# Four edits to the weight conversion and the attention steps in the first token group of an attention and MoE kernel

## The chip, the cores and the metric

The kernel runs on one core of a Trainium2 chip. The metric is device time in microseconds (us), from one launch that does everything, as the median of several runs.

## The reference

Linear attention with decay runs over blocks of 64 tokens, for 4 batches and 8 heads of 64 features; its output, laid out as 3072 tokens by 512 features, then goes through a two-layer network with a squared ReLU.

```python
for b in range(nb):                      # nb = 768 / 64 blocks
    intra = einsum('bhic,bhjc->bhij', qb, kb) * Dmask       # lam ** (i - j), lower triangle
    intra = einsum('bhij,bhjd->bhid', intra, vb)
    inter = einsum('bhid,bhde->bhie', qb * lam_pow, kv_state)
    out[:, :, sl] = intra + inter
    kv_state = lam_block * kv_state + einsum('bhsd,bhse->bhde', kb * rev_pow, vb)
x = out.transpose(0, 2, 1, 3).reshape(3072, 512)
h = x @ w_in                             # 512 x 2048
g = maximum(h, 0) ** 2
return g @ w_out                         # 2048 x 512
```

## The kernel before, in words

Attention works in chunks t of 128 tokens (24 of them, 6 to a batch), each with two blocks of 64. The network works in token groups m of four chunks (512 tokens). All matrix products of the network are taken in three parts, from a rounded upper and a remaining lower part of each factor: weights `wh` and `wl`, inputs `xh` and `xl`, squared activations `gh` and `gl`.

The order of the instructions of each engine is written out by hand: what the code says first, an engine does first, and it waits there when its input is not ready. Only the order between engines is left to semaphores.

The program has four stages. A prologue does the attention of chunks 0 to 3. Then token group m = 0 runs 16 steps f = 0 to 15. In step f, TensorE (PE) computes `hidden(0, f)` (12 matmuls, L587), then `project` of the step before (12 matmuls, L623 to L628). Meanwhile the weights of slot u = f + 2 are converted on the fly, since they come from memory as 64-bit words that have to be split in two: `first_hi` and `first_lo` on ScalarE (ACT, L210 and L215) write a working buffer `A`; `clamp`, `shift`, `sign` and `rounded` on VectorE (DVE, L223, L227, L234, L240) turn it into the rounded weight; `upper` (ACT, L246) copies it to `wh`; `lower` (DVE, L249) subtracts that from `A` and writes `wl`. `A` has two buffers, used in turn by slots.

The activations of a step go from PSUM through ACT: `positive` (L594) and two squares (L598, L603); then `rest` (DVE, L608) writes `gl`, and with it the PSUM bank of that step's h comes free.

In every fourth step (f = 2, 6, 10, 14; step 2 of four) PE also does a `burst` between `hidden` and `project`: it computes the scores of chunk t + 1, the results of chunk t and the new state terms of chunk t + 1, all as small 64 x 64 matmuls (L386), into one bank of `h` and two banks b0 and b1. `masked` (DVE, L477 or L484) multiplies scores by the decay mask and writes `a`; `keep` copies results into xh and xl of the next group; `fade` (ACT, L514, four instructions) multiplies the old state by the decay; `advance` (DVE, L300 with st) adds the new term from PSUM onto it, once for each block b of the chunk. The chain of a chunk is advance(t, 0), fade(t, 1), advance(t, 1). Chunk 4 is the first in this loop. Its scores and terms stand in `att`, two banks that `look` fills at the end of step 0. Those banks are given back before step 2, and b0 and b1 of burst(5) take their place.

GpSimd (POOL) scales k and q (`prep_k`, L471; `prep_q`, L466). `turn` (L256) is a one-element copy on POOL that reads a piece of `wl` that DVE has just written, and so holds POOL until then. SyncE (SP) issues the loads: `wload(u)` for the raw weights, `load_kq` and `load_v` for a chunk.

After m = 0 come m = 1 and two pairs of groups with seven products in place of eight; nothing of the weight conversion is left there.

Of the kernel before, what the change touches and what calls it, by code (L numbers as in the profile page):

```python
# [7 lines left out]
F32 = mybir.dt.float32  # L8
# [7 lines left out]
P = 128  # L16
# [6 lines left out]
DM = H * D  # L23
# [19 lines left out]
def body(ctx: ExitStack, tc: tile.TileContext, qT, kT, kvq, lam, w, out):  # L43
    nc = tc.nc
    const = ctx.enter_context(tc.tile_pool(name="const", bufs=1))
    dram = ctx.enter_context(tc.tile_pool(name="dram", bufs=1, space=bass.MemoryType.DRAM))
    wk = ctx.enter_context(tc.tile_pool(name="wk", bufs=2))
    small = ctx.enter_context(tc.tile_pool(name="small", bufs=1))
# [27 lines left out]
    def warm(n):  # L76
        w_ = two_banks(ps_a, "att")
        for _ in range(n):
            nc.tensor.matmul(  # L79
                w_[:, 0], st[:, 0, 0].rearrange("p a b -> p (a b)"),  # L80
                st[:, 0:2].rearrange("p n c a b -> p (n c a b)"), start=True, stop=True,
            )

    warm(4)

# [85 lines left out]

    wh = const.tile([P, 2 * NF, DM], F32R, name="wh")
    wl = const.tile([P, 2 * NF, DM], F32R, name="wl")

# [8 lines left out]

    raw, cv, hole = {}, {}, None

# [21 lines left out]
    def first_hi(u):  # L207
        r = raw.pop(u).bitcast(U32).rearrange("p (n two) -> p n two", two=2)
        A = wk.tile([P, r.shape[1]], U32, name="A")
        nc.scalar.activation(A.bitcast(F32), r[:, :, 1].bitcast(F32), AF.Abs)  # L210
        cv[u] = r[:, :, 0], r[:, :, 1], A

# [29 lines left out]
    def flat(t, u):  # L242
        return t[:, pieces(u)].rearrange("p a b -> p (a b)")

    def upper(u):
        nc.scalar.copy(flat(wh, u), cv[u][2].bitcast(F32))  # L246

    def lower(u):
        V.tensor_tensor(  # L249
            out=flat(wl, u), in0=cv.pop(u)[2].bitcast(F32), in1=flat(wh, u).bitcast(F32),  # L250
            op=ALU.subtract,
        )

# [6 lines left out]
    for t in range(4):  # L260
        place(t)
        load_kf(t)
        load_all(t)
    wload(1)

# [202 lines left out]
    def prep_k(t):  # L468
        x = chunk[t]["k"]
        y = near.rearrange("p j a c -> p a j c")[:, :, :, T - 1 : T]  # L470
        nc.gpsimd.tensor_tensor(out=x, in0=x, in1=y.broadcast_to([P, NPR, 2, D]), op=ALU.mult)  # L471

    def masked(t):
# [9 lines left out]
        for j in range(2):  # L483
# [4 lines left out]
            )  # L488

    def before_block(n):  # L490
        return st[:, n % 3]

# [175 lines left out]
    def w_parts(i, S):  # L668
        p1, p2 = w_in(2 * i), w_in(2 * i + 1)
        hl = wk.tile([P, 2, 4, HALF], F32R, name="hl", tag="raw")  # L670
        nc.scalar.copy(hl[:, 0], S)
        V.tensor_tensor(out=hl[:, 1], in0=S, in1=hl[:, 0].bitcast(F32), op=ALU.subtract)
        for k, x in enumerate((wh, wl)):
            x = x.bitcast(F32)
            nc.sync.dma_start(
                out=wd[i, :, W11 : W12 + 1, k], in_=x[:, p1].rearrange("p (b n) -> p b n", b=2)
            )
            nc.sync.dma_start(out=wd[i, :, W22, k], in_=x[:, p2, HALF:DM])
            nc.sync.dma_start(out=wd[i, :, WS1 : WS4 + 1, k], in_=hl[:, k].bitcast(F32))
# [174 lines left out]
    copy_qx(2)  # L854
    first_hi(1)
    low[0]()
    load(4)
    load_vx(4)
    early(1, banks())
# [8 lines left out]
    copy_vx(3)  # L868
    low[1]()
    early_news(3)  # L870
    masked(3)
    upper(0)
    copy_qx(3)
    early(2, banks())
    wload(2)
    low[2] = split(2, o[2])
    clamp(1)
    state(3)
    lower(0)
# [22 lines left out]
    for m in range(PLAIN):  # L902
# [6 lines left out]
        for f in range(NF):  # L909
            h = hidden(m, f, *xs_of[m])  # L910
            if m == 0:
# [213 lines left out]
```

## Time and profile before

| | us |
|---|---|
| median of 3 runs | 589.23 (588.75 to 589.6) |
| the profiled execution, its own time | 588.08 |
| its span in the trace | 586.2 |
| PE busy | 572.8 (98%) |
| DVE busy | 323.1 (55%) |
| ACT busy | 317.5 (54%) |
| POOL busy | 66.7 (11%) |

All times below are microseconds from the start of the span. PE's matmuls overlap: one of 128 x 512 is drawn as 0.39 long, and the next starts about 0.23 after it. DVE's and ACT's drawn lengths overlap the next instruction by some 0.06 to 0.1, so the distance between two starts is the price of an instruction. What stands in brackets behind a row is the idle time ahead of it on its engine and what ended it.

### The profile page before, as it was taken

How to read it: one execution, taken by the hardware profiler on the slowest of the kernel's cores; microseconds unless marked ns; L12 is line 12 of the kernel's file. 1: busy time of each engine (PE TensorE's matmuls, PEld its weight loads, DVE VectorE, ACT ScalarE, POOL GpSimd, SP SyncE). 2: the span in 40 equal slices, each digit the busy share in tenths (PEclk: the TensorE clock that was granted, in tenths of full speed). 3: DMA queues.
4: the chain of work that ended last, by engine and by line, in shares of the span. 5: the costliest groups of instructions: out<-in, count | busy, mean ns of one | idle time of the engine just before them, and what ended most of it. 6: DMA issues, size and time to landing. Idle time of an engine off the chain costs nothing.

```text
span 586.2 us, 12793 instructions
## 1 busy us (share of the span) xinstructions
PE 572.8 (98%) x5240; PEld 470.1 (80%) x5240; DVE 323.1 (55%) x587; ACT 317.5 (54%) x594; POOL 66.7 (11%) x87
## 2 busy tenths in 40 slices
PE   8899999999999999999999999999999999999997
PEld 5777887788888888888888888888888888888885
DVE  6899999975767776534344343446433333334222
ACT  3698887976665465445545445634344444444221
POOL 7401202033232000011111101000000000000000
PEclk8999999999999999999999999999999999999999
DMA  8676667346797933856554553300354444411001
GB/s 335 220 283 228 223 217 229 104 128 196 243 364 260 348 130 103 284 164 197 168 166 137 179 173 98 126 1 0 102 168 126 125 122 120 122 50 73 1 0 72
DMA packets 52089, 93.62 MB, mean 160 GB/s; under 512 B 4672, under 2 KB 19520, under 8 KB 52032
## 3 DMA queue, kind: packets, MB, share of 16 engines
q1 hardware_dynamic: 52032, 92.82, 49.5%
q8 instruction: 41, 0.67, 0.4%
q14 instruction: 16, 0.13, 0.1%
HBM read 71.83 MB, written 20.97 MB: 158 GB/s over the span
## 4 chain that ended last, share of the span: by engine, by line
PE 87%; DVE 6%; ACT 3%; issue 2%; DMA 1%; POOL 1%; POOLq 0%; DVEq 0%
PE h L729 26%; PE acc L623 14%; PE acc L628 14%; PE acc L624 13%; PE h L587 11%; PE h L386 4%; PE b L386 3%; DVE A L234 1%; PE att L79 1%; DVE wl L249 1%; DVE A L240 1%; ACT A L210 1%; DVE A L227 1%; DVE A L223 1%; DVE st L500 1%
## 5 line engine op out<-in xcount | busy, mean ns | idle before, releaser
L623 PE MATMUL acc<-wh,gh 128*128 128x512 f32 x384 | 151.7, 395 | 0.0
L624 PE MATMUL acc<-wl,gh 128*128 128x512 f32 x384 | 149.6, 389 | 0.0
L628 PE MATMUL acc<-wh,gl 128*128 128x512 f32 x384 | 149.3, 390 | 0.1
L623 PEld LDWEIGHTS acc<-wh,gh 128*128 128x128 f32 x384 | 72.1, 188 | 16.0 <-issue 0.3
L628 PEld LDWEIGHTS acc<-wh,gl 128*128 128x128 f32 x384 | 72.1, 188 | 15.2
L624 PEld LDWEIGHTS acc<-wl,gh 128*128 128x128 f32 x384 | 72.1, 188 | 14.4
L608 DVE TENSOR_TENSOR gl<-h,gh 128x512 fp32r<-128x512 f32 x48 | 33.1, 689 | 69.7 <-ACT h L603 69.7
L594 ACT ACTIVATE h<-h 128x512 f32<-128x512 f32 x48 | 28.1, 584 | 69.7 <-PE h L587 36.0
L300 DVE TENSOR_TENSOR temp<-h,temp 128x512 f32<-128x512 f32 x48 | 33.0, 688 | 56.9 <-PE h L729 46.8
L729 PE MATMUL h<-wh,ring 128*128 128x512 f32 x224 | 60.0, 390 | 0.0
L594 ACT ACTIVATE temp<-temp 128x512 f32<-128x512 f32 x16 | 10.1, 632 | 88.6 <-DVE temp L300 88.6
L729 PEld LDWEIGHTS h<-wh,ring 128*128 128x128 f32 x224 | 42.0, 188 | 8.9 <-DVE r L300 0.3
L466 POOL TENSOR_TENSOR qs<-set,qpow 128x512 f32<-128x512 f32 (+1 forms) x21 | 26.5, 1260 | 170.7 <-PE b L386 159.2
L587 PE MATMUL h<-xh,wh 128*128 128x512 f32 x128 | 34.6, 392 | 3.0 <-DVE a L484 2.2
L300 DVE TENSOR_TENSOR r<-h,temp 128x512 f32<-128x512 f32 x24 | 16.6, 692 | 34.2 <-PE h L729 33.1
L608 DVE TENSOR_TENSOR gl<-r,gh 128x512 fp32r<-128x512 f32 x24 | 16.6, 690 | 32.9 <-ACT gh L761 32.9
L729 PE MATMUL h<-wl,ring 128*128 128x512 f32 x112 | 34.5, 389 | 0.0
L587 PE MATMUL h<-xh,wl 128*128 128x512 f32 x128 | 34.5, 391 | 0.0
L587 PE MATMUL h<-xl,wh 128*128 128x512 f32 x128 | 34.3, 389 | 0.0
L761 ACT CAST gh<-r 128x512 fp32r<-128x512 f32 x24 | 14.9, 621 | 30.0 <-PE acc L624 30.0
L587 PEld LDWEIGHTS h<-xh,wh 128*128 128x128 f32 x128 | 23.7, 188 | 9.0 <-ACT gh L598 3.0
L729 PE MATMUL h<-wh 128*128 128x512 f32 x112 | 30.1, 390 | 0.0
(180 smaller groups left out, 1040.1 us busy)
## 6 DMA issues: line engine op xcount, KB each, us to landing
ring<-wd SPq DMA_DIRECT2D x56, 256.0 KB, 2.9
raw<-in_w SPq DMA_DIRECT2D x22, 512.0 KB, 4.7
set<-in_kvq SPq DMA_DIRECT2D x19, 512.0 KB, 3.8
wd<-hl SPq DMA_DIRECT2D x16, 512.0 KB, 5.0
wh<-wd SPq DMA_DIRECT2D x28, 256.0 KB, 2.9
wl<-wd SPq DMA_DIRECT2D x28, 256.0 KB, 2.8
set<-in_kT SPq DMA_DIRECT2D x22, 256.0 KB, 4.2
set<-in_w SPq DMA_DIRECT2D x10, 512.0 KB, 4.9
```

What stands on the lines that cost most here:

```text
L79: nc.tensor.matmul(w_[:, 0], st[:, 0, 0].rearrange("p a b -> p (a b)"), st[:, 0:2].rearrange("p n c a b -> p (n c a b)"), start=True, stop ...
L300: lambda o, x, y, op=op: V.tensor_tensor(out=o, in0=x, in1=y, op=op)
L386: nc.tensor.matmul(self.banks[row][rows[col], at : at + D], lhsT, rhs, start=key not in self.begun, stop=stop, skip_group_check=True,)
L466: nc.gpsimd.tensor_tensor(out=z, in0=x, in1=w_, op=ALU.mult)
L587: nc.tensor.matmul(h, wt[:, w_in(f), kt * P : (kt + 1) * P], x[:, kt], start=k == 0, stop=k == 11)
L594: nc.scalar.activation(h, h, AF.Relu)
L608: V.tensor_tensor(out=gl, in0=r, in1=gh.bitcast(F32), op=ALU.subtract)
L623: nc.tensor.matmul(accs[m][i], gh[:, cs], wh[:, j], start=f == 0, stop=False)
L624: nc.tensor.matmul(accs[m][i], gh[:, cs], wl[:, j], start=False, stop=False)
L628: nc.tensor.matmul(accs[m][i], gl[:, cs], wh[:, j], start=False, stop=end)
L729: nc.tensor.matmul(bank, w[:, kw * HALF + kt * P : kw * HALF + (kt + 1) * P], x_slot(2 * c + kt, kx), start=first and q == 0, stop=q == 5, ...
L761: nc.scalar.copy(gh, r_of[f])
```

## The change

It has these parts:

- In step 2, `masked(t + 1)` follows `keep` of the same step; before, it stood in step 3, behind `lower`.
- In step f = 1, the loads of chunk 5 are followed by `wload(5)`, which stood ahead of them in step 0. `advance(4, 0)` moves from the front of the step to behind `turn`, and `advance(4, 1)` from step 1 to step 2, behind `lower`.
- In steps 1 and 2 of four, from f = 2 on, `lower` is shared: DVE does the first 512 columns, POOL the second 512 behind a `turn`.
- A third buffer for `A`, used by every third slot; it lies where the last pieces of `wl` are put later (`late`, `wlz`, `whz`).
- In step 2, the copies of qx go to step 3.
- In the prologue, some states of the attention are written to a spare half of `A` (`aside`); `upper(0)`, `lower(0)` and `first_hi(1)` stand earlier, `clamp(1)` and `load_vx(4)` later; `wload(1)` is issued ahead of chunks 2 and 3; `warm` has 3 matmuls where it had 4.

```diff
-    warm(4)
+    warm(3)
...
     def first_hi(u):
         r = raw.pop(u).bitcast(U32).rearrange("p (n two) -> p n two", two=2)
-        A = wk.tile([P, r.shape[1]], U32, name="A")
+        if u % 3 == 2 and u < NLOT - 2:
+            if not third:
+                third.append(late.tile([P, 2 * NF - EARLY, DM], U32, name="third", tag="wl"))
+            A = third[0].rearrange("p a b -> p (a b)")[:, 0 : 2 * DM]
+        else:
+            A = wk.tile([P, 2 * DM], U32, name="A")
+        if u == 0:
+            beside.append(A[:, DM : 2 * DM].bitcast(F32))
+        A = A[:, 0 : r.shape[1]]
...
-    def lower(u):
-        V.tensor_tensor(
-            out=flat(wl, u), in0=cv.pop(u)[2].bitcast(F32), in1=flat(wh, u).bitcast(F32),
-            op=ALU.subtract,
-        )
+    def lower(u, shared=False):
+        x, h, A = flat(wl, u), flat(wh, u).bitcast(F32), cv.pop(u)[2].bitcast(F32)
+        n = DM if shared else x.shape[1]
+        V.tensor_tensor(out=x[:, 0:n], in0=A[:, 0:n], in1=h[:, 0:n], op=ALU.subtract)
+        if shared:
+            turn(u)
+            nc.gpsimd.tensor_tensor(out=x[:, n:], in0=A[:, n:], in1=h[:, n:], op=ALU.subtract)
...
-    wload(1)
+        if t == 1:
+            wload(1)
...
+    aside = {3: 0, 4: 1, 7: 0}
+
     def before_block(n):
-        return st[:, n % 3]
+        if n in aside:
+            x = beside[0][:, aside[n] * 4 * D : (aside[n] + 1) * 4 * D]
+            return x.rearrange("p (a j d) -> p a j d", a=2, j=2)
+        return st[:, {5: 0, 6: 1}.get(n, n % 3)]
...
     prep_k(1)
+    upper(0)
     copy_vx(0)
     masked(0)
+    lower(0)
     early_news(0)
     state(0)
     copy_qx(0)
     first_scores(1, banks())
     prep_q(1)
+    first_hi(1)
...
-    first_hi(1)
     low[0]()
     load(4)
-    load_vx(4)
...
-    low[1]()
     early_news(3)
     masked(3)
-    upper(0)
+    low[1]()
...
-    clamp(1)
     state(3)
-    lower(0)
     early(3, banks())
+    load_vx(4)
     wload(3)
     low[2]()
     low[3] = split(3, o[3])
+    clamp(1)
     low[3]()
...
                 if f == 1:
                     load_kq(t + 1)
                     load_v(t + 1)
-                if f == 1:
+                    wload(u_ + 2)
                     masked(t)
-                    advance(t, 0)
                 if u_ < NLOT:
...
-                    lower(u_ - 1)
-                if f:
+                    lower(u_ - 1, step in (1, 2))
+                if f == 1 or f and step in (0, 3):
                     turn(u_ - 1)
...
                 if f == 1:
+                    advance(t, 0)
                     fade(t, 1)
+                if f == 2:
                     advance(t, 1)
                 if step == 3:
                     fade(t + 1, 0)
-                    masked(t + 1)
                     advance(t + 1, 0)
...
                     rounded(u_)
-                    wload(u_ + 3)
+                    if f:
+                        wload(u_ + 3)
...
                 if step == 2:
                     keep(t, x)
-                    if t + 1 == 2 * G:
-                        copy_vx(t + 1)
+                    masked(t + 1)
+                if step == 3:
                     copy_qx(t + 1)
                 if f == NF - 1:
+                    copy_vx(t + 1)
                     fade(t + 1, 1)
                     advance(t + 1, 1)
```

The first place is DVE in steps f = 1 and f = 2, around clamp(3) and rest(1), in the program before. `st<-att` are the advances of chunk 4; both stand ahead of rest(1) (the `gl` row), one ahead of clamp(3).

```order
L300 TENSOR_TENSOR st<-att,st 128x256 [waits Activation_49]
L223 TENSOR_SCALAR A<-A 128x1024
L249 TENSOR_TENSOR wl<-A,wh 128x1024 [waits Activation_49]
L227 TENSOR_SCALAR A<-A 128x1024 [waits DVE_49]
L234 SCALAR_TENSOR_TENSOR A<-set_93,A 128x1024 [waits DMAHW3_49,DMAHW4_49,DMAHW2_49,DMAHW5_49,DVE_49,Pool_49]
L300 TENSOR_TENSOR st<-att,st 128x256 [waits Activation_49]
L240 ISA A<-set_93,A 128x2048 [waits DVE_49]
L608 TENSOR_TENSOR gl<-h,gh 128x512 [waits Activation_49,Pool_49]
```

The same part of DVE in the changed program, up to the second advance, with clamp at L252, shift at L256, sign at L263, rounded at L269, lower at L283, advance at L335 and rest at L649.

```order
L252 TENSOR_SCALAR A<-A 128x1024
L283 TENSOR_TENSOR wl<-third,wh 128x1024
L256 TENSOR_SCALAR A<-A 128x1024
L263 SCALAR_TENSOR_TENSOR A<-set_95,A 128x1024
L335 TENSOR_TENSOR st<-att,st 128x256
L269 ISA A<-set_95,A 128x2048
L649 TENSOR_TENSOR gl<-h,gh 128x512
L252 TENSOR_SCALAR A<-A 128x1024
L256 TENSOR_SCALAR A<-A 128x1024
L263 SCALAR_TENSOR_TENSOR A<-raw,A 128x1024
L283 TENSOR_TENSOR wl<-A,wh 128x512
L335 TENSOR_TENSOR st<-att,st 128x256
```

advance(4, 0) has moved from ahead of clamp(3) to behind sign(3), and advance(4, 1) from ahead of rounded(3) to behind the shared lower(3), that is behind rest(1), clamp(4), shift(4) and sign(4). On ACT the order has stayed: after upper(2) (the first row here) come the four instructions of fade(4, 1), and behind them positive(1), the squares of step 1, the copies of qx and first_hi(4).

```order
L278 CAST wh<-third 128x1024
L555 ACTIVATE st<-st,fd 128x64 x4
L635 ACTIVATE h<-h 128x512
L639 ACTIVATE gh<-h 128x512
L644 ACTIVATE h<-h 128x512
L171 COPY qx<-qs 64x256 x2
L239 ACTIVATE A<-set_95 128x1024
```

The third place is PE at the front of burst(5), in step f = 2, before the change: the last matmuls of hidden(2), then the scores, in turn into a bank of h and into b1. The first waits for DVE (rest(1), which gives the h bank back); the second waits for nothing outside PE.

```order
L587 MATMUL h<-xl,wh 128x512 x4
L386 MATMUL h<-set_92 64x64 [waits DMAHW1_49,DMAHW0_49,DVE_49]
L386 MATMUL b_777<-set_92 64x64 [waits PE_49]
L386 MATMUL h<-set_92 64x64
L386 MATMUL b_777<-set_92 64x64
```

The same rows in the changed program.

```order
L628 MATMUL h<-xl,wh 128x512 x4
L421 MATMUL h<-set_94 64x64 [waits DMAHW7_49,DMAHW6_49,DVE_49]
L421 MATMUL b_778<-set_94 64x64 [waits DVE_49,PE_49]
L421 MATMUL h<-set_94 64x64
L421 MATMUL b_778<-set_94 64x64
```

The second matmul now waits for DVE too. The instruction that it waits for is the last reader of the old `att` banks, advance(4, 1).

## Rows read from the trace of the kernel before

**Rows 1.** The page's busy time by engine, and PE's waits over the whole span (in total, times, longest).

```profile
PE 572.8 (98%) x5240; PEld 470.1 (80%) x5240; DVE 323.1 (55%) x587; ACT 317.5 (54%) x594; POOL 66.7 (11%) x87
...
PE h L587 <- DVE a L484: 2.2, 2, 1.4
...
PE h L386 <- DVE gl L608: 1.3, 1, 1.3
...
PE b L386 <- ACT mark L441: 0.2, 1, 0.2
```

**Rows 2.** The timeline of PE: the last matmuls of hidden(2) and the first of burst(5); the last of project(2) and the first of hidden(4); the first of hidden(12); the first of project(12). The first number is the start, the second the length.

```profile
41.48 1.07 PE L587 MATMUL h<-xl,wh 128*128 128x512 f32 x4
43.88 0.27 PE L386 MATMUL h<-set 64*64 64x64 f32 x1 [1.32 <-DVE gl L608]
...
53.98 0.39 PE L628 MATMUL acc<-wh,gl 128*128 128x512 f32 x1
55.77 1.15 PE L587 MATMUL h<-xh,wh 128*128 128x512 f32 x4 [1.40 <-DVE a L484]
...
105.76 1.17 PE L587 MATMUL h<-xh,wh 128*128 128x512 f32 x4 [0.84 <-DVE a L484]
...
114.04 0.39 PE L623 MATMUL acc<-wh,gh 128*128 128x512 f32 x1
```

**Rows 3.** Busy time by stretch of the span: stretch, its length, then PE, PEld, DVE, ACT and POOL (busy us, instructions), the granted clock of PE as a share of 2.4 GHz, the DMA engines' share and GB/s.

```profile
10.00:15.00 5.00, 4.07 (x106) 3.72 (x109) 3.23 (x8) 3.13 (x11) 4.54 (x6) 0.56 1.02 416
15.00:20.00 5.00, 4.69 (x217) 4.42 (x217) 3.42 (x12) 3.64 (x9) 3.27 (x3) 0.76 0.75 274
...
40.00:50.00 10.00, 8.68 (x142) 7.13 (x141) 9.84 (x11) 7.86 (x16) 2.96 (x4) 1.00 0.73 257
...
122.00:586.00 464.00, 459.70 (x3776) 379.72 (x3774) 210.57 (x407) 221.26 (x428) 37.04 (x33) 1.00 0.46 142
```

**Rows 4.** The timeline of ACT: first_hi(2); then, from 37.53 on, upper(2), fade(4, 1), positive(1), its squares, the copies of qx, first_hi(4), first_lo(4), upper(3).

```profile
29.81 1.17 ACT L210 ACTIVATE A<-raw 128x1024 f32<-128x1024 f32 x1 [2.69 <-DMA raw<-in_w]
...
37.53 1.05 ACT L246 CAST wh<-A 128x1024 fp32r<-128x1024 f32 x1
38.47 1.08 ACT L514 ACTIVATE st<-st,fd 128x64 f32<-128x64 f32 x4
39.43 0.59 ACT L594 ACTIVATE h<-h 128x512 f32<-128x512 f32 x1
40.06 0.60 ACT L598 ACTIVATE gh<-h 128x512 fp32r<-128x512 f32 x1
40.55 0.59 ACT L603 ACTIVATE h<-h 128x512 f32<-128x512 f32 x1
41.17 0.83 ACT L169 COPY qx<-qs 64x256 f32<-64x256 f32 x2
42.03 1.15 ACT L210 ACTIVATE A<-raw 128x1024 f32<-128x1024 f32 x1
43.09 1.13 ACT L215 ACTIVATE raw<-raw 128x1024 uint32<-128x1024 uint32 x1
44.10 1.03 ACT L246 CAST wh<-A 128x1024 fp32r<-128x1024 f32 x1
```

**Rows 5.** The timeline of DVE: lower(0), half as wide as the others; then, from 38.61 on, lower(2), shift(3), sign(3), advance(4, 1), rounded(3), rest(1), clamp(4); then rest(2) and rounded(4); at last rest(12).

```profile
25.72 0.68 DVE L249 TENSOR_TENSOR wl<-A,wh 128x512 fp32r<-128x512 f32 x1
...
38.61 1.23 DVE L249 TENSOR_TENSOR wl<-A,wh 128x1024 fp32r<-128x1024 f32 x1
39.75 0.69 DVE L227 TENSOR_SCALAR A<-A 128x1024 uint32<-128x1024 uint32 x1
40.53 1.22 DVE L234 SCALAR_TENSOR_TENSOR A<-set,A 128x1024 uint32<-128x1024 uint32 x1
41.67 0.41 DVE L300 TENSOR_TENSOR st<-att,st 128x256 f32<-128x256 f32 x1
42.01 1.22 DVE L240 CUSTOM_DVE_ANT_0 A<-set,A 128x2048 uint16<-128x2048 uint16 x1
43.14 0.68 DVE L608 TENSOR_TENSOR gl<-h,gh 128x512 fp32r<-128x512 f32 x1
43.74 1.01 DVE L223 TENSOR_SCALAR A<-A 128x1024 f32<-128x1024 f32 x1
...
47.79 0.68 DVE L608 TENSOR_TENSOR gl<-h,gh 128x512 fp32r<-128x512 f32 x1
48.39 2.12 DVE L240 CUSTOM_DVE_ANT_0 A<-raw,A 128x2048 uint16<-128x2048 uint16 x1
...
113.12 0.68 DVE L608 TENSOR_TENSOR gl<-h,gh 128x512 fp32r<-128x512 f32 x1
```

**Rows 6.** The timeline of POOL: turn(2), prep_k(5), prep_q(5).

```profile
39.90 0.57 POOL L256 COPY mark<-wl 1x1 f32<-1x1 f32 x1 [16.42 <-DVE wl L249]
43.15 1.06 POOL L471 TENSOR_TENSOR set<-set,near 128x512 f32<-128x512 f32 x1 [2.67 <-DMA set<-in_kvq]
...
48.14 1.28 POOL L466 TENSOR_TENSOR qs<-set,qpow 128x512 f32<-128x512 f32 x1
```

**Rows 7.** The timeline of SP's queue: the issue of the raw weights of slots 4 and 5, and the first load of chunk 5.

```profile
30.85 6.46 SPq L201 DMA_DIRECT2D raw<-in_w  x4
37.41 0.39 SPq L147 DMA_DIRECT2D set<-in_kvq  x1
```

More of the change, by code (lines that the diff above doesn't have):

```diff
@@ L37 @@
 RING = 8
+EARLY = 2 * NF - 3
 SUMS = (1, 2, 3, 5, 6, 7, 9, 11)
@@ L46, in body @@
     dram = ctx.enter_context(tc.tile_pool(name="dram", bufs=1, space=bass.MemoryType.DRAM))
+    late = ctx.enter_context(tc.tile_pool(name="late", bufs=1))
     wk = ctx.enter_context(tc.tile_pool(name="wk", bufs=2))
@@ L169, in copy_qx, with __init__, open, __getitem__ @@
             nc.scalar.copy(chunk[t]["qx"][r, :, n], chunk[t]["qs"][rows[1 - y], 2 * y : 2 * y + 2, n])
-    wh = const.tile([P, 2 * NF, DM], F32R, name="wh")
-    wl = const.tile([P, 2 * NF, DM], F32R, name="wl")
+    class Weights:
+        def __init__(self, name):
+            self.name = name
+            self.main = const.tile([P, EARLY, DM], F32R, name=name)
+            self.last = None
+        def open(self):
+            self.last = late.tile([P, 2 * NF - EARLY, DM], F32R, name=self.name + "z", tag=self.name)
+        def __getitem__(self, key):
+            p, j, *rest = key
+            if isinstance(j, slice):
+                x, j = (self.main, j) if j.start < EARLY else (
+                    self.last, slice(j.start - EARLY, j.stop - EARLY))
+            else:
+                x, j = (self.main, j) if j < EARLY else (self.last, j - EARLY)
+            return x[(p, j, *rest)]
+    wh, wl = Weights("wh"), Weights("wl")
     def w_in(f):
@@ L182, in pieces @@
         return slice(max(2 * u - 1, 0), min(2 * u + 1, 2 * NF))
-    raw, cv, hole = {}, {}, None
+    raw, cv, hole, beside, third = {}, {}, None, [], []
     def wload(u):
@@ L208, in first_hi @@
         r = raw.pop(u).bitcast(U32).rearrange("p (n two) -> p n two", two=2)
-        A = wk.tile([P, r.shape[1]], U32, name="A")
+        if u % 3 == 2 and u < NLOT - 2:
+            if not third:
+                third.append(late.tile([P, 2 * NF - EARLY, DM], U32, name="third", tag="wl"))
+            A = third[0].rearrange("p a b -> p (a b)")[:, 0 : 2 * DM]
+        else:
+            A = wk.tile([P, 2 * DM], U32, name="A")
+        if u == 0:
+            beside.append(A[:, DM : 2 * DM].bitcast(F32))
+        A = A[:, 0 : r.shape[1]]
         nc.scalar.activation(A.bitcast(F32), r[:, :, 1].bitcast(F32), AF.Abs)
@@ L245, in upper @@
     def upper(u):
+        if u == NLOT - 2:
+            wh.open()
+            wl.open()
         nc.scalar.copy(flat(wh, u), cv[u][2].bitcast(F32))
-    def lower(u):
-        V.tensor_tensor(
-            out=flat(wl, u), in0=cv.pop(u)[2].bitcast(F32), in1=flat(wh, u).bitcast(F32),
-            op=ALU.subtract,
-        )
+    def lower(u, shared=False):
[5 more added lines that the diff above has]
+            nc.gpsimd.tensor_tensor(out=x[:, n:], in0=A[:, n:], in1=h[:, n:], op=ALU.subtract)
     def turn(u):
@@ L673, in w_parts @@
         for k, x in enumerate((wh, wl)):
-            x = x.bitcast(F32)
             nc.sync.dma_start(
-                out=wd[i, :, W11 : W12 + 1, k], in_=x[:, p1].rearrange("p (b n) -> p b n", b=2)
+                out=wd[i, :, W11 : W12 + 1, k],
+                in_=x[:, p1].bitcast(F32).rearrange("p (b n) -> p b n", b=2),
             )
-            nc.sync.dma_start(out=wd[i, :, W22, k], in_=x[:, p2, HALF:DM])
+            nc.sync.dma_start(out=wd[i, :, W22, k], in_=x[:, p2, HALF:DM].bitcast(F32))
             nc.sync.dma_start(out=wd[i, :, WS1 : WS4 + 1, k], in_=hl[:, k].bitcast(F32))
```

## The prediction

> **What bounds the kernel now.** I read the page's busy times first: PE is busy for 98% of the span, and after 122 us it works 459.7 of 464 us with no wait in its list [rows 1, 3]. So what a step of the first 122 us gains or loses for PE comes out at the end, one to one. The list of PE's waits comes second: `a` from DVE's masking holds it twice for 2.2 us together, the `gl` of rest(1) once for 1.3, ACT's `mark` once for 0.2 [rows 1]. The timeline of PE tells where: ahead of burst(5) at 43.88, of hidden(4) at 55.77, of hidden(12) at 105.76 [rows 2]. Why PE waits there is read from the busy times by stretch: from 40 to 50 us DVE is busy for 9.84 of 10 [rows 3], since it converts the weights. At rest(12), which starts at 113.12 and whose `gl` project(12) needs, PE arrives at 114.04 [rows 2, 5], almost on DVE's heels. So two engines run neck and neck until step 12: DVE by its own queue, PE by what it is held up.
>
> **Masking in step 2.** PE has work for hidden(4) from 54.21 on (53.98 and 0.23 more) and starts at 55.77; 1.56 us are lost. At 105.76 it is 0.84 idle plus the 0.16 by which the last matmul is drawn too long, 1.0; `mark` is 0.2 plus 0.16, 0.4. With the first group of matmuls at each restart 0.1 longer (1.15 and 1.17 against 1.07 for the same four) that makes 3.2 us [rows 1, 2]. Masking behind `keep` takes it away, as far as DVE is no later than PE then. This is the most that the change can give behind burst(5).
>
> **The two advances of chunk 4.** Here the change adds a chain. In the order, advance(4, 0) stands behind sign(3) now. ACT's fade(4, 1) needs its result and stands in ACT's queue ahead of positive(1), so everything behind it on ACT waits. Step by step:
> - Before, fade(4, 1) started at 38.47, right behind upper(2) [rows 4]. Now advance(4, 0) takes the place at 41.67 that advance(4, 1) had, with 0.41, since lower(2), shift(3) and sign(3) in front of it hang on upper(2) (38.58) and have their old lengths [rows 4, 5]. fade starts at 42.1: 3.6 later.
> - From fade's start to positive(1) it is 0.96, to the first square 0.63, to the second 0.49, and this one takes 0.59 [rows 4]. The squares of step 1 end at 44.8. rest(1), which started at 43.14, starts at 44.8 and is done at 45.4. DVE idles in front of it, from 43.14 on.
> - The copies of qx (0.86 to the next start) and first_hi(4) (1.15) follow on ACT [rows 4], so first_hi(4) ends at 46.8. clamp(4) needs it, and stood at 43.74.
> - Behind clamp(4) (0.7, as its sister shift has 0.69; the 1.01 is beside POOL) come shift(4) 0.72, sign(4) 1.15, the half lower(3) 0.6 (the half-wide lower(0) is drawn as 0.68) and advance(4, 1) 0.4 [rows 5, 6]. It ends at 50.4. upper(3), moved from 44.10 to 47.7, is in time.
> - The second matmul of burst(5) waits for that instruction, because b1 lies in the bank that it reads. All the rest of PE's queue is behind it: the burst, project(1), hidden(3). Before, it went on at 43.88 [rows 2]; now at 50.4. PE loses **6.5 us**, and idles from 42.6 for nearly 8 us, with one small matmul at 45.4.
>
> Against the 3.2 that this makes up for (PE is so late afterwards that the masks, rest(3) and rest(12) are in time), 3.3 remain. For the check: rest(2) now waits for `mark` behind the burst and two squares, to about 52.2, 4.4 later than 47.79 [rows 5]; DVE regains 1 us of that in idle time that it no longer has, and reaches rest(12) some 3.3 later; PE reaches project(12) 3.3 later too. So it stays with PE, if DVE gains nothing or a little.
>
> **Chunk 5 sent for sooner.** Its loads were issued at 37.41, behind the four raw loads that take the queue from 30.85 on [rows 7], and prep_k(5) started when they landed, at 43.15 [rows 6]. Now they stand ahead of wload(5), so prep_k(5) finds its data and follows turn(2). turn(2) waited for shift(3) and ended at 40.47, just ahead of sign(3) at 40.53 [rows 5, 6]. What it costs when the two meet, a row shows: rounded(4) at 48.39 took 2.12 where rounded(3) took 1.22, while prep_q(5) ran from 48.14 to 49.42 [rows 5, 6]. If POOL comes first, sign(3) and everything in the chain above is 0.95 later; if sign comes first, rounded(3) pays, whose time is hidden by the idle time ahead of rest(1). Bounds 0 to 0.95; turn's end lies ahead of sign's start, so I take **0.95**. The Trainium skill says the same of the cause ("SBUF — State Buffer", Who interferes with whom): DVE and GpSimd share a port pair, by an exclusive lock; the trace agrees.
>
> **Half of `lower` on POOL.** Seven times DVE saves 1.14 less 0.6, 3.8 us together [rows 5]. POOL's half reads two operands from SBUF as prep_k does (1.06) [rows 6], and can hold up a DVE instruction by 0.9 as above. So per half DVE gains 0.5 or loses 0.4; over the five halves ahead of step 12 between -2.7 and +2. I take no change: DVE's gain is no gain for PE, which is later than DVE already; its loss counts beyond about 0.7.
>
> **Third buffer, qx copies, prologue.** The buffer takes away waits of first_hi for `lower`; on the chain above first_hi(4) is set by fade, so 0. The qx copies leave ACT sooner in step 2 and are hidden by PE's lateness. In the prologue lower(0), 0.6 [rows 5], goes ahead of the first states, warm loses one matmul, and the separate states let DVE go on sooner: -0.5 to +0.9, and I take **+0.2**. The first_hi(2), from which ACT runs without a gap, is set by the landing of raw(2) at 29.81 after 2.69 idle [rows 4], so nothing is gained there.
>
> **The clock.** In the prologue the granted clock fell to half: 0.56 from 10 to 15 us, 0.76 from 15 to 20; at full speed 5 x 0.44 + 5 x 0.24 = 3.4 us of PE's work [rows 3]. At the waits of 1.3 and 1.4 us it did not fall [rows 2, 3]. The new one of nearly 8 us is longer than any. Half speed costs only while PE works again: 0 to 3.4; I take **1.2**, as part of it passes in the wait. The Trainium skill ("TensorE: Matmul & The Clock Gate", Part 1) says that an idle engine goes back to 1.2 GHz and rises only after it has been busy for a while, which speaks for a loss; no row here shows it for a wait of that length. By the rule the 1.2 stands in the sum, without it the sum is 1.2 less.
>
> **The sum.** 6.5 - 3.2 + 0.95 + 0.2 + 1.2 = +5.65. The profiled execution took 588.08, 1.15 less than the median; its stretches serve for the difference, so 588.08 + 5.65 = 593.7 for an execution like it, and 589.23 + 5.65 = 594.9 for the median.
>
> **Rivals.**
> 1. The chain, but without the clock's fall or without the meeting of prep_k(5) and sign(3): 589.23 + 3.5 = 592.7 with neither, 593.7 and 593.9 with one. For it: the clock stayed full at 1.4 us of idle. Against it: the wait is five times longer.
> 2. POOL keeps the port at each half, and DVE is last at rest(12): 2 more, less 0.7 of slack, so about 596.2. For it: 2.12 for rounded(4). Against it: rests and clamps lie between, which give POOL time.
> 3. Not slower: ACT's chain runs sooner. Its place is first_hi(2), where ACT idles 2.69 for raw(2) [rows 4]. If the new order of the loads lets raw(2) land that much sooner, upper(2), sign(3) and the fade come up to 2.7 sooner, and burst(5) goes on at 47.7: 589.23 + 0.6 + 0.2 = 590.0. From 3.5 us of lead on nothing is lost, and with burst(5) held up no longer than before, the whole 3.2 would be gained, 586. Against it: raw(2) is sent for when a buffer of the prologue comes free, which the change leaves in its place.
>
> **How the numbers follow.** The forecast (chain, meeting and some loss of clock) has 0.5, rival 1 0.25, rival 2 0.08, rival 3 0.17. A measurement of this kernel tells about 0.2%, 1.2 us, from no change. Rival 3 gives 0.08 of faster and 0.09 of same; the others are slower, 0.83. The range goes from 590.5, just above rival 3 at its likeliest, to 597.5: the forecast with the clock's full 3.4 (597.1) and a little for rival 2.
>
> **What would show it.** Right: PE's list of waits has one for advance's `st` of 4 to 6 us at an L421 matmul of burst(5), one for `gl` ahead of it; fade(4, 1) stands at about 42 with idle time ahead of it; the waits for `a` are gone; the granted clock is below 1 somewhere between 43 and 55. Wrong: fade(4, 1) before 40, or PE waiting again behind burst(5), at project(12) above all; then DVE, not PE, is what ends late.

## The result, and the profile after

The changed kernel takes 596.37 us (median of 4 runs, 595.70 to 597.55) where the kernel before takes 588.99 (588.63 to 589.60): a ratio of 1.0126, with a 95% interval from 1.0108 to 1.0145. It is 7.4 us slower. The forecast was 594.9, in a range from 590.5 to 597.5. The profiled execution after took 596.29, with a span of 594.4.

The list of PE's waits after (in total, times, longest) answers to [rows 1]:

```profile
PE b L421 <- DVE st L335: 4.5, 1, 4.5
PE h L421 <- DVE gl L649: 4.0, 1, 4.0
...
PE h L628 <- ACT wh L278: 1.0, 1, 1.0
PE h L628 <- DVE wl L283: 0.9, 2, 0.5
```

The waits for `a` and for `mark` are gone. Two new ones of 4.0 and 4.5 us stand at L421, in the burst; the one for `wh` and the longer of the two for `wl` stand ahead of them, at hidden(1). The timeline of PE (start, length, and in brackets the idle time ahead and what ended it) shows both in burst(5), then the first matmul of project(1), and a later wait of hidden(12):

```profile
48.31 0.47 PE L421 MATMUL h<-set 64*64 64x64 f32 x2 [3.98 <-DVE gl L649]
...
53.25 0.33 PE L421 MATMUL b<-set 64*64 64x64 f32 x1 [4.47 <-DVE st L335]
...
56.80 0.50 PE L664 MATMUL acc<-wh,gh 128*128 128x512 f32 x1
...
114.81 1.20 PE L628 MATMUL h<-xh,wl 128*128 128x512 f32 x4 [0.44 <-DVE wl L283]
```

Before, the burst went through from 43.88 [rows 2]. Now its first matmuls wait for rest(1), and the first one into b1, 4.9 us later, for advance(4, 1). The timeline of ACT tells why rest(1) is late: first_hi(2), upper(2), fade(4, 1), positive(1), the squares of step 1, the copies of qx, first_hi(4).

```profile
31.66 1.12 ACT L239 ACTIVATE third<-raw 128x1024 f32<-128x1024 f32 x1 [4.44 <-DMA raw<-in_w]
...
39.31 1.06 ACT L278 CAST wh<-third 128x1024 fp32r<-128x1024 f32 x1
44.79 1.06 ACT L555 ACTIVATE st<-st,fd 128x64 f32<-128x64 f32 x4 [4.43 <-DVE st L335]
45.76 0.58 ACT L635 ACTIVATE h<-h 128x512 f32<-128x512 f32 x1
46.37 0.60 ACT L639 ACTIVATE gh<-h 128x512 fp32r<-128x512 f32 x1
46.86 0.59 ACT L644 ACTIVATE h<-h 128x512 f32<-128x512 f32 x1
47.48 0.83 ACT L171 COPY qx<-qs 64x256 f32<-64x256 f32 x2
48.34 1.12 ACT L239 ACTIVATE A<-raw 128x1024 f32<-128x1024 f32 x1
```

ACT stands still for 4.43 us in front of fade(4, 1), which followed upper(2) without a gap before [rows 4]. What it waits for is advance(4, 0) on DVE. DVE's timeline, from sign(3) to rest(2), is the other half of the chain:

```profile
42.32 2.04 DVE L263 SCALAR_TENSOR_TENSOR A<-set,A 128x1024 uint32<-128x1024 uint32 x1
44.29 0.41 DVE L335 TENSOR_TENSOR st<-att,st 128x256 f32<-128x256 f32 x1
44.62 1.21 DVE L269 CUSTOM_DVE_ANT_0 A<-set,A 128x2048 uint16<-128x2048 uint16 x1
47.56 0.69 DVE L649 TENSOR_TENSOR gl<-h,gh 128x512 fp32r<-128x512 f32 x1 [1.73 <-ACT h L644]
49.49 0.69 DVE L252 TENSOR_SCALAR A<-A 128x1024 f32<-128x1024 f32 x1 [1.24 <-ACT A L239]
...
52.09 0.69 DVE L283 TENSOR_TENSOR wl<-A,wh 128x512 fp32r<-128x512 f32 x1
52.69 0.42 DVE L335 TENSOR_TENSOR st<-att,st 128x256 f32<-128x256 f32 x1
55.72 0.69 DVE L649 TENSOR_TENSOR gl<-h,gh 128x512 fp32r<-128x512 f32 x1 [2.61 <-ACT h L644]
```

DVE, 9.84 of 10 us busy in that stretch before [rows 3], now idles 1.73, 1.24 and 2.61 us for ACT. sign(3) took 2.04 where it took 1.22 [rows 5]; POOL's timeline shows turn(2) and prep_k(5) beside it:

```profile
41.69 0.58 POOL L290 COPY mark<-wl 1x1 f32<-1x1 f32 x1 [17.49 <-DVE wl L283]
42.23 1.05 POOL L506 TENSOR_TENSOR set<-set,near 128x512 f32<-128x512 f32 x1
```

Busy times in three stretches after (PE, PEld, DVE, ACT, POOL, then the granted clock) show what the wait does to PE's clock: 0.50 in the wait and all through the burst, 1.00 only behind it.

```profile
46.50:53.20 6.70, 0.47 (x2) 0.29 (x2) 4.24 (x6) 5.32 (x8) 0.29 (x2) 0.50 0.49 158
53.20:56.60 3.40, 3.35 (x109) 3.38 (x110) 0.88 (x2) 1.61 (x4) 1.48 (x2) 0.50 0.03 7
56.70:60.00 3.30, 3.30 (x19) 2.68 (x17) 3.30 (x6) 3.09 (x4) 0.80 (x1) 1.00 0.48 131
```

The account, in the spans of the two profiled executions: the first matmul of burst(5) into b1 is at 53.25 instead of 43.88, and PE is 9.4 us later. From there to project(1) it takes 3.55 us, against about 2 before (43.88 to 45.90), 1.5 more by the clock. Of the 3.2 to 3.5 us of waits that the kernel before had behind burst(5), nothing is left; some 1.1 of new ones stand around 114.81, since PE comes onto DVE's heels again (from the first matmul of hidden(12) and hidden(13) to that of the project behind it are 3.46 and 3.08 us, and 2.72 where PE doesn't wait). 9.4 + 1.5 - 3.4 + 1.1 = 8.6; the spans differ by 8.2.

### The profile page after: what moved, and what is told of

The parts are those of the page before. It is cut to its first block, busy times and chain, and to the rows that moved or that the text cites. A ratio compares the mean times of both kernels' runs of the same rounds, so it can differ in the third digit from the quotient of the medians.

```text
span 594.4 us, 12781 instructions
## 1 busy us (share of the span) xinstructions
PE 573.8 (97%) x5238; PEld 471.8 (79%) x5238; DVE 323.7 (54%) x587; ACT 318.1 (54%) x594; POOL 78.1 (13%) x94
## 4 chain that ended last, share of the span: by engine, by line
PE 86%; DVE 7%; issue 4%; DMA 1%; ACT 1%; POOL 0%; POOLq 0%; SPq 0%; DVEq 0%; ACTq 0%
PE h L770 26%; PE acc L664 14%; PE acc L669 14%; PE acc L665 14%; PE h L628 11%; PE h L421 4%; PE b L421 3%; DVE A L263 1%; DVE A L252 1%; DMA set<-in_kvq 1%; DVE A L269 1%; DVE wl L283 1%; DVE gl L649 1%; DVE A L256 0%; DVE third L263 0%
## 5 line engine op out<-in xcount | busy, mean ns | idle before, releaser
L664 PE MATMUL acc<-wh,gh 128*128 128x512 f32 x336 | 132.7, 395 | 0.0
L669 PE MATMUL acc<-wh,gl 128*128 128x512 f32 x336 | 130.9, 390 | 0.1
L665 PE MATMUL acc<-wl,gh 128*128 128x512 f32 x336 | 130.9, 389 | 0.0
L664 PEld LDWEIGHTS acc<-wh,gh 128*128 128x128 f32 x336 | 63.0, 188 | 14.0 <-issue 0.3
L669 PEld LDWEIGHTS acc<-wh,gl 128*128 128x128 f32 x336 | 63.1, 188 | 13.3
L665 PEld LDWEIGHTS acc<-wl,gh 128*128 128x128 f32 x336 | 63.1, 188 | 12.7
L649 DVE TENSOR_TENSOR gl<-h,gh 128x512 fp32r<-128x512 f32 x48 | 33.1, 689 | 71.9 <-ACT h L644 71.9
L635 ACT ACTIVATE h<-h 128x512 f32<-128x512 f32 x48 | 27.9, 582 | 71.8 <-PE h L628 38.1
L335 DVE TENSOR_TENSOR temp<-h,temp 128x512 f32<-128x512 f32 x48 | 33.0, 688 | 56.9 <-PE h L770 47.0
L501 POOL TENSOR_TENSOR qs<-set,qpow 128x512 f32<-128x512 f32 (+1 forms) x21 | 28.9, 1377 | 173.2 <-PE b L421 161.4
L335 DVE TENSOR_TENSOR r<-h,temp 128x512 f32<-128x512 f32 x24 | 16.6, 692 | 34.5 <-PE h L770 33.3
L649 DVE TENSOR_TENSOR gl<-r,gh 128x512 fp32r<-128x512 f32 x24 | 16.6, 690 | 32.9 <-ACT gh L802 32.9
L628 PE MATMUL h<-xl,wh 128*128 128x512 f32 x120 | 32.1, 389 | 0.0
L639 ACT ACTIVATE gh<-h 128x512 fp32r<-128x512 f32 x48 | 28.8, 599 | 1.4
L644 ACT ACTIVATE h<-h 128x512 f32<-128x512 f32 x48 | 28.5, 594 | 0.0
```

What stands on the lines that cost most here:

```text
L335: lambda o, x, y, op=op: V.tensor_tensor(out=o, in0=x, in1=y, op=op)
L501: nc.gpsimd.tensor_tensor(out=z, in0=x, in1=w_, op=ALU.mult)
L628: nc.tensor.matmul(h, wt[:, w_in(f), kt * P : (kt + 1) * P], x[:, kt], start=k == 0, stop=k == 11)
L635: nc.scalar.activation(h, h, AF.Relu)
L639: nc.scalar.activation(gh, h, AF.Square)
L644: nc.scalar.activation(h, h, AF.Square)
```

## The experiments

The theory: the two advances of chunk 4, put later, hold first ACT's fade(4, 1) and then the bank of b1, and PE's half clock adds to it. The rivals: the halves on POOL and the port; the loads; the prologue. All medians below stand beside runs of the kernel before on the same chip (588.78 to 589.04 on three chips).

The profiles begin first_hi(2) at different times, from 29.81 to 32.83, and each kernel was profiled in one execution. So the text also gives, for the profiled execution, the time from the start of first_hi(2) to the first matmul of project(13), which leaves the prologue out: 91.84 us before, 98.45 after. What follows project(13) takes 463.7 to 465.0 us in all the profiles.

**Both advances back** in the changed kernel, all else kept:

```diff
                     wload(u_ + 2)
                     masked(t)
+                    advance(t, 0)
...
                 if f == 1:
-                    advance(t, 0)
                     fade(t, 1)
-                if f == 2:
                     advance(t, 1)
```

> The changed kernel with both advances of chunk 4 put back where they stood before (advance(4,0) right behind masked(4), advance(4,1) in step 1 behind fade(4,1)); all other parts of the change stay. Theory (the advances hold ACT's fade and burst(5)): the wait of 4.5 us for the advance's st and the granted clock below 1 between 40 and 60 us are gone; burst(5) starts at about 46.5 and goes on at once, since raw(2) still lands 1.9 us late and sign(3) still meets prep_k(5); 587 to 590 us. Rival 1 (GpSimd's halves and the port cost it): stays at 594 to 597. Rival 2 (the late landing of raw(2) is the cause): stays above 592.

Measured: 589.70 us, ratio 1.0012 (0.9996 to 1.0028). 6.7 of the 7.4 us are gone. PE's one wait at burst(5) in this run, from its list:

```profile
PE h L421 <- DVE gl L649: 2.1, 1, 2.1
```

and fade(4, 1) in the timeline of ACT:

```profile
31.89 1.12 ACT L239 ACTIVATE third<-raw 128x1024 f32<-128x1024 f32 x1 [4.39 <-DMA raw<-in_w]
...
40.47 1.08 ACT L555 ACTIVATE st<-st,fd 128x64 f32<-128x64 f32 x4
```

The wait for the advance is gone, and the fade is back right behind upper(2). From first_hi(2) to project(13) it takes 91.34 us, 7.1 less than after. The 0.9 that is left is what the gains and losses of all other parts come to together, and its interval reaches 0.

**One advance at a time.** First only advance(4, 0) back, which frees the fade and leaves the bank held:

```diff
                     masked(t)
+                    advance(t, 0)
...
                 if f == 1:
-                    advance(t, 0)
                     fade(t, 1)
                 if f == 2:
                     advance(t, 1)
```

> The changed kernel with only advance(4,0) put back behind masked(4); advance(4,1) stays in step 2 behind the half lower(3). Theory: fade(4,1) follows upper(2) at about 40.4 again, rest(1) starts near 45.4 instead of 47.6, and burst(5) goes on at about 49.7 instead of 53.25; the clock may or may not fall; 591.0 to 594.0 us. If the fade did not matter: as the changed kernel, 596.4.

Measured: 593.01 us, ratio 1.0064 (1.0041 to 1.0086). Its timeline of PE:

```profile
44.58 0.32 PE L421 MATMUL h<-set 64*64 64x64 f32 x2 [1.94 <-DVE gl L649]
48.20 0.34 PE L421 MATMUL b<-set 64*64 64x64 f32 x1 [3.29 <-DVE st L335]
```

fade(4, 1) starts at 38.58, right behind upper(2) again. This execution was an early one (first_hi(2) at 29.97, 591.55 us), so its rows stand 1 to 2 us ahead of the expected ones.

Then only advance(4, 1) back, which frees the bank and leaves the fade late:

```diff
                 if f == 1:
                     advance(t, 0)
                     fade(t, 1)
-                if f == 2:
                     advance(t, 1)
```

> The changed kernel with only advance(4,1) put back into step 1, right behind fade(4,1); advance(4,0) stays behind sign(3). Theory: rest(1) still starts at about 47.6 because ACT's squares are late, but the bank of b1 is free by then, so burst(5) runs through from about 48.3; one wait of 4 us instead of two; 589.5 to 592.5 us. If the bank's wait did not matter: 596.4.

Measured: 592.41 us, ratio 1.0058 (1.0039 to 1.0078). Its rows of PE and ACT:

```profile
49.22 0.37 PE L421 MATMUL h<-set 64*64 64x64 f32 x1 [3.94 <-DVE gl L649]
...
45.71 1.06 ACT L555 ACTIVATE st<-st,fd 128x64 f32<-128x64 f32 x4 [4.42 <-DVE st L335]
```

This execution was a late one (first_hi(2) at 32.59), so the burst stands 0.9 behind the expected 48.3.

Each of the two moves costs by itself: over the run with both back, the late advance(4, 1) 3.3 us and the late advance(4, 0) 2.7, together 6.0 of the 6.7. From first_hi(2) to project(13) the profiles have 95.14 and 94.48 us against 91.34, that is 3.8 and 3.1, together 6.9 of 7.1. Both links of the chain are thus shown apart.

**The two moves alone**, in the kernel before:

```diff
                     masked(t)
-                    advance(t, 0)
...
                 if f == 1:
-                    fade(t, 1)
-                    advance(t, 1)
+                    advance(t, 0)
+                    fade(t, 1)
+                if f == 2:
+                    advance(t, 1)
```

> The kernel before with only the two advances of chunk 4 moved as the change moves them (advance(4,0) behind sign(3), advance(4,1) in step 2 behind lower(3), which is whole here). Theory: fade(4,1) starts at 42.1, rest(1) at 44.8, burst(5) goes on at about 51.0; the clock falls for some us; the wait for a at hidden(4) is gone as PE is late; 592.5 to 596 us. Rivals 1 and 2 (halves, or raw(2)): 588.5 to 590, since neither is in it.

Measured: 595.29 us, ratio 1.0110 (1.0088 to 1.0132): 6.5 us slower than before with nothing else of the change. (From first_hi(2) to project(13): 97.86, 6.0 more than before. A wait for `a` of 0.2 is left.) Its timeline has the same rows, and first_hi(2):

```profile
52.08 0.34 PE L386 MATMUL b<-set 64*64 64x64 f32 x1 [5.16 <-DVE st L300]
...
43.09 1.07 ACT L514 ACTIVATE st<-st,fd 128x64 f32<-128x64 f32 x4 [3.61 <-DVE st L300]
...
30.78 1.12 ACT L210 ACTIVATE A<-raw 128x1024 f32<-128x1024 f32 x1 [4.57 <-DMA raw<-in_w]
```

The last row matters too: with the old order of the loads, ACT idles 4.57 us for raw(2) here, as in the changed kernel (4.44), and 2.69 in the profile before [rows 4]. A long wait for raw(2) comes without the change; the start of first_hi(2) is 1.0 later than before here, and 1.9 later in the changed kernel.

**The clock**: 40 more filler matmuls in the wait of the changed kernel, so that PE isn't idle. They compute nothing that is used.

```diff
-        for _ in range({1: 10, 2: 6}.get(f, 0) if m == 0 else 0):
+        for _ in range({1: 10, 2: 46}.get(f, 0) if m == 0 else 0):
```

> The changed kernel with 46 instead of 6 filler matmuls ahead of hidden(2), that is 40 more of 0.227 us, 9.1 us together, put into the time in which PE waits at burst(5); the order and all waits stay. Theory (the half clock costs 1.6 us at the burst, which took 3.55 us instead of 1.93): PE is busy until about 53.3, the granted clock stays 1.0 between 40 and 60 us, the burst takes about 2 us; 594.3 to 595.4 us. Rival (the clock costs nothing, since PE is caught up with by DVE later): 596 to 597.

Measured: 594.56 us, ratio 1.0089 (1.0057 to 1.0121), 1.8 less than the changed kernel. Busy times and clock in two stretches of this run:

```profile
40.00:50.00 10.00, 10.00 (x45) 8.28 (x45) 6.38 (x7) 5.47 (x12) 1.58 (x2) 1.00 0.55 189
50.00:60.00 10.00, 10.00 (x148) 8.27 (x147) 7.59 (x13) 7.88 (x15) 2.70 (x3) 1.00 0.23 68
```

The clock stays at 1.00, and the burst takes 2.0 us (53.52 to 55.55) instead of 3.55. From first_hi(2) to project(13) it is 97.08, 1.4 less than in the changed kernel. So the half clock has a price, 1.4 to 1.8; the two intervals of the medians overlap, and the burst's 1.5 in the traces is the firmest of the three figures.

**load_vx(4) back as well** (both advances back):

```diff
     load(4)
+    load_vx(4)
     early(1, banks())
...
     early(3, banks())
-    load_vx(4)
     wload(3)
```

> The changed kernel with both advances of chunk 4 back, and load_vx(4) back in its old place ahead of wload(2), so that it isn't sent for between wload(2) and wload(3). Theory (load_vx(4) behind wload(2) is what lets raw(2) land 1.9 us later): raw(2) lands at 29.5 to 30.2, hidden(1) no longer waits 1.0 for upper(1), everything up to step 12 is earlier by up to 1.8; 587.5 to 588.8 us. Rival (the landing is late for another reason): 589.5 as with the advances alone.

Measured: 589.37 us, ratio 1.0007 (0.9991 to 1.0022), no different from the run without it. ACT idled 3.45 for raw(2), less than 4.4, but the whole prologue of the profiled execution was later, and raw(2) landed at 32.4. The expectation that raw(2) would land before 30.2 failed. From the issue of raw(2) at 26.52 to first_hi(2) it is 5.9 us here and 6.3 to 6.9 in the profiles with load_vx(4) behind wload(2); but with the whole prologue as before, load_vx(4) included, it is 5.1 to 7.2, so the place of load_vx(4) isn't shown to set it.

**wload(5) ahead of chunk 5 again** (both advances back):

```diff
                     load_v(t + 1)
-                    wload(u_ + 2)
...
                     rounded(u_)
-                    if f:
-                        wload(u_ + 3)
+                    wload(u_ + 3)
```

> The changed kernel with both advances of chunk 4 back, and wload(5) ahead of chunk 5's loads again (in step 0). Theory (prep_k(5) meets sign(3) and costs 0.8): prep_k(5) starts when its data lands, after 44 us, sign(3) takes 1.2 instead of 2.0, burst(5) starts near 45.9; DVE pays some of it at clamp(4); 588.5 to 589.5 us. Rival (the meeting is made up for behind it): 589.7.

Measured: 588.16 us, ratio 0.9983 (0.9966 to 1.0000), 1.5 less than with the new order. In this run sign(3) is free of POOL, and prep_k(5) starts when its data has landed, beside clamp(4). The rows of ACT, DVE and POOL:

```profile
30.65 1.13 ACT L239 ACTIVATE third<-raw 128x1024 f32<-128x1024 f32 x1 [4.15 <-DMA raw<-in_w]
...
41.34 1.23 DVE L263 SCALAR_TENSOR_TENSOR A<-set,A 128x1024 uint32<-128x1024 uint32 x1
...
43.76 1.19 POOL L506 TENSOR_TENSOR set<-set,near 128x512 f32<-128x512 f32 x1 [2.48 <-DMA set<-in_kvq]
```

Only a part of the 1.5 is the meeting's. first_hi(2), which stands ahead of both places of wload(5), starts at 30.65 here and at 31.89 in the run with both advances back; from there to project(13) it takes 90.80 against 91.34 us, 0.5 less. Why this execution started earlier, and the medians differ by as much, isn't settled.

**lower whole on DVE** (both advances back):

```diff
-                    lower(u_ - 1, step in (1, 2))
-                if f == 1 or f and step in (0, 3):
+                    lower(u_ - 1)
+                if f:
                     turn(u_ - 1)
```

> The changed kernel with both advances of chunk 4 back, and with lower whole on DVE in all steps (no half on POOL). Theory of the prediction (a half gives DVE 0.5 and costs it up to as much by the port, so that the halves are worth nothing): the same as with the halves, 589.2 to 590.5 us. Rival (the halves are worth their 0.54 each, and DVE is what binds behind burst(5)): 2.0 to 3.0 more, 591.5 to 592.7. Rival (the port costs more than it gives): 587 to 589.

Measured: 589.13 us, ratio 0.9999 (0.9985 to 1.0013), against 589.70 with the halves: worth nothing. From first_hi(2) to project(13) it is 91.32 without and 91.34 with them. The run with the halves shows why, in clamp(8) on DVE beside the half of lower(6) and prep_k on POOL; the last row is clamp(8) in the run without halves, beside prep_k alone:

```profile
69.92 2.35 DVE L252 TENSOR_SCALAR third<-third 128x1024 f32<-128x1024 f32 x1
...
69.41 1.29 POOL L286 TENSOR_TENSOR wl<-A,wh 128x512 fp32r<-128x512 f32 x1
70.67 1.05 POOL L506 TENSOR_TENSOR set<-set,near 128x512 f32<-128x512 f32 x1
...
71.52 1.10 DVE L252 TENSOR_SCALAR third<-third 128x1024 f32<-128x1024 f32 x1
```

clamp takes 0.69 alone, 1.10 beside prep_k and 2.35 here: it ends only behind both POOL instructions, which follow each other without a gap. clamp(12) takes 2.33 with the half and 1.09 without, and rounded(8) 2.12 and 1.57; rounded(4) and rounded(12) are as long either way. So DVE loses 3.0 us over the five halves ahead of step 12, where they save it 5 x 0.54 = 2.7.

**Masking in step 2 alone**, in the kernel before:

```diff
                     fade(t + 1, 0)
-                    masked(t + 1)
                     advance(t + 1, 0)
...
                     keep(t, x)
+                    masked(t + 1)
```

> The kernel before with only the masking moved into step 2 behind keep. Theory (DVE is right ahead of PE at every step, so the 3.2 us of waits for a can't be gained): the waits for a are gone from PE's list, but waits for rest's gl or lower's wl of nearly the same size come up later, and the end moves by at most the slack of 0.7 at project(12); 588.2 to 589.0 us against 589.0. Rival (the waits for a are lost time of PE): 585.6 to 586.2 us.

Measured: 587.43 us, ratio 0.9979 (0.9965 to 0.9992). It is the one part of the change that gains by itself, 1.6 us, more than the 0 to 0.8 expected and half of the 3.2 that PE waited for. From first_hi(2) to project(13) it takes 90.77 us, 1.1 less than before. Two of PE's waits now:

```profile
PE h L587 <- DVE wl L249: 0.7, 2, 0.5
...
PE b L386 <- ACT mark L441: 0.3, 1, 0.3
```

The waits for `a` are gone. Of the two for `wl`, one (0.45 at 34.26) stands ahead of the first mask that was moved; behind it 0.29 at 56.21 came up. That DVE gives back a part of the gain is right; the slack of 0.7 was sized too small.

**The steps without the prologue's part**: both advances, wload(5) and the whole prologue as before (the diff of the change in reverse in these places), so that masking, halves, third buffer and qx copies are left.

> The changed kernel with both advances of chunk 4, the order of wload(5) and chunk 5, and the whole prologue (order, warm(4), wload(1), states) as before; what is left of the change is masking in step 2, the halves on POOL, the third buffer and the qx copies. Theory (the prologue's part costs PE 0.5 to 1 by a wait for pz ahead of near, and nothing is gained by its states): 587.0 to 588.2 us, some 0.5 less than 588.2 with the new prologue. Rival (the prologue's part is a gain): 588.6 or more.

Measured: 588.32 us, ratio 0.9989 (0.9977 to 1.0001), the same as 588.16 with the new prologue, to about 1.2 us by the two intervals. No gain or loss of the prologue's part is seen. And the same with lower whole on DVE:

> As the run with the steps alone, and lower whole on DVE. What is left is masking in step 2, the third buffer and the qx copies. Theory (the halves are worth next to nothing, since POOL's half holds up a DVE instruction): within 0.8 us of the run with the halves. Rival (the halves are worth 0.54 each and DVE binds): 2 to 3 us slower than that run.

Measured: 587.75 us, ratio 0.9977 (0.9963 to 0.9992), 0.6 less than with the halves, as in the pair above. With masking alone at 587.43, the third buffer and the qx copies give nothing that can be seen. The profiles say it more sharply: from first_hi(2) to project(13) it is 90.82 us with the steps alone, 90.74 without the halves, and 90.77 with masking alone, so the masking is all that these steps gain.

**Four warm matmuls** in place of three (advances and wload(5) back, new prologue):

```diff
-    warm(3)
+    warm(4)
```

> The changed kernel with the advances and wload(5) back, and four warm matmuls ahead of near in place of three. Theory (with three, PE waits 0.5 to 1.8 us for pz, and the clock of the first 10 us falls below 1 in some executions): no wait for pz, the granted clock from 0 to 10 us is 1.0; 587.4 to 588.2 us against 588.2 with three. Rival (the start doesn't matter, as the fetch of instructions at 23.8 us sets the end of the prologue): 588.2.

Measured: 590.52 us, ratio 1.0029 (1.0015 to 1.0043), 2.4 more than with three: neither of the two expectations. A wait for `pz` is left as well (0.4, against 0.5 with three). From first_hi(2) to project(13) it is 90.82 us, as with three (90.80), but first_hi(2) starts at 32.83 instead of 30.65. PE's timeline has the time in the prologue:

```profile
21.35 0.40 PE L421 MATMUL open<-rest,st 64*64 64x64 f32 x12 [1.73 <-issue]
25.27 0.40 PE L421 MATMUL open<-raw,A 64*64 64x64 f32 x13 [1.83 <-issue]
```

In two places of the same small matmuls PE waits for nothing that another engine does. Why one more matmul at the start makes these waits longer isn't settled.

## Why the prediction was right, point by point

**The chain of the advances** held link by link. It was forecast that fade(4, 1) starts at 42.1, rest(1) at 44.8, clamp(4) at 46.8 and that burst(5) goes on at 50.4, all 0.95 later with the meeting of sign(3) and prep_k(5). Measured are 44.79, 47.56, 49.49 and 53.25. Each is 1.7 to 1.9 behind the forecast with the meeting, and the first row of the chain already is: first_hi(2) stands at 31.66 instead of 29.81. The durations that the steps were built from were right; the start was that of one execution.

**That start** is the term that was set at 0 and came out as 1.9 in the trace. But the new order of the loads isn't shown to be its cause. raw(2) was sent for at nearly the same time in the profiles before and after:

```profile
24.67 0.81 SPq L201 DMA_DIRECT2D raw<-in_w  x2
...
24.72 1.91 SPq L222 DMA_DIRECT2D raw<-in_w  x2
```

first_hi(2) started 5.1 us behind that issue before, and 6.9 after; in the other twelve profiles, four of them with the old order, it is 5.9 to 7.2. The profile before was an execution with an early landing, and its 588.08 against a median of 589.2 fits that, as it does that the spans differ by 8.2 and the medians by 7.4.

**The clock** was taken at 1.2, between 0 and 3.4; it costs 1.5 in the trace, and 1.4 (trace) to 1.8 (medians) by the experiment. The rule cited from the Trainium skill ("TensorE: Matmul & The Clock Gate", Part 1), that an idle engine goes back to 1.2 GHz, is borne out for this wait: the rows show 0.50 from 46.5 to 56.6.

**The meeting of sign(3) and prep_k(5)** was taken at 0.95; sign(3) is 2.04 against 1.22, 0.82 more. Undone, it gave 0.5 between first_hi(2) and project(13), so a part was made up for behind it; the 1.5 of the medians has more in it than the meeting (with the two intervals, that difference is known to about 1.5).

**The gain of the masking** was sized as 3.2, if PE is late enough. In the changed kernel nothing was left of these waits, so that held; but 1.1 of new waits for `wl` came up late, which the forecast put at none. The step that failed there is the check at rest(12): it gave DVE the idle time back and took the halves as neutral, but looked at `gl` alone. What PE needs first is the lower part of the weights, at the fifth matmul of a hidden, as the row at 114.81 shows.

**The halves** were taken as no change, between -2.7 and +2: 0.6 less without them in medians, nothing in the traces behind first_hi(2). **The prologue** was taken at +0.2: 588.16 against 588.32, nothing that the runs can tell.

**The sum.** In medians the two moves alone cost 6.5 (595.29 against 588.78), and the rest of the change 0.9 (589.70, with an interval that reaches 0), together the 7.4 that were measured; 5.65 were forecast. In the traces 6.6 stand between first_hi(2) and project(13) (98.45 against 91.84), where the forecast had 5.45, its sum without the prologue's 0.2. What is missing there are the late waits of 1.1, which had no term, and the clock's term, 0.2 to 0.6 too small. The other 0.8 of the 7.4, if the traces stand for the medians, lies ahead of first_hi(2), and what costs it isn't settled. It was luck in part that 596.37 lies inside the range: its top came from the room that was left for the clock and rival 2, not from the late waits.

Rival 2, that POOL keeps the port and DVE ends last, is seen in part (clamp at 2.35), but its price is small. Rival 3, an earlier raw(2), didn't come: it was later.

Masking in step 2 alone, without the other parts, beats both kernels: 587.43 us.

## What to carry to other kernels

An instruction that is moved to give its own engine room has to be followed to everyone who waits for it: here a 0.4 us addition stood at the head of another engine's queue and was the last reader of a bank, and both together held TensorE for 8.5 us. When an engine is that close behind another, removing its longest wait gives at most the distance to the next thing that the other engine owes it, so look for the earliest use (here the weights' lower part), not for the one that the list of waits names. And the start of a chain read from one execution can be off by more than the effects that are added to it, so compare two traces from an event behind the part that varies: from first_hi(2) to project(13), five kernels whose medians spread over 3.1 us agreed within 0.1.

## What the runs showed of the hardware

- The same wait of 2.1 us at burst(5) left PE's clock full in one kernel's profile and halved it in another's. Busy times and granted clock from 48 to 52 us, first with both advances back, then with lower whole on DVE as well. In the second it fell behind the end of the wait: the burst began at 47.26, and the clock was 1.00 up to 48, 0.79 from 48 to 49 and 0.50 from 49 to 51.

```profile
48.00:52.00 4.00, 4.00 (x54) 3.38 (x47) 3.98 (x4) 3.57 (x6) 2.02 (x3) 1.00 0.68 258
```

```profile
48.00:52.00 4.00, 4.00 (x83) 3.50 (x74) 3.97 (x5) 3.77 (x8) 0.94 (x2) 0.57 0.76 281
```

- The half clock in the prologue [rows 3] goes with a later end of it. In seven profiles with the same new prologue, hidden(0) started at 25.2 and 25.5 us where the granted clock from 10 to 20 us was 0.66, at 26.2 to 26.6 where it was 0.54 or 0.55, and at 27.2 in both where it was 0.50. With the old prologue it was 25.2 and 25.8 at 1.00, 26.0 and 26.5 at 0.83, and 26.1 at 0.66. That the clock is the cause isn't shown. The stretch in the runs of the two moves alone, of advance(4, 0) back and of advance(4, 1) back:

```profile
10.00:20.00 10.00, 6.69 (x330) 5.96 (x326) 6.36 (x20) 7.37 (x20) 7.59 (x7) 1.00 1.01 387
```

```profile
10.00:20.00 10.00, 8.60 (x327) 7.93 (x325) 8.00 (x27) 8.07 (x21) 7.21 (x7) 0.66 0.98 384
```

```profile
10.00:20.00 10.00, 8.84 (x243) 8.34 (x246) 6.48 (x18) 7.27 (x18) 6.56 (x8) 0.50 0.80 305
```

- GpSimd held a DVE instruction up over two of its own that followed each other (2.35 us, against 1.10 beside one of them and 0.69 beside none), and not just until the first was done.
